# Three small moves in a TensorE-bound kernel: q of one more batch by DMA transpose, 1/rms of three batches spread by a DRAM round trip, and a new instruction order

## The chip, the cores and the metric

The kernel runs on one core of one Trainium2 chip. The metric is the device time of one execution in microseconds (us), the median over several runs. Each run also has a span (first to last instruction in the profile) and a mean granted TensorE clock. The profile of one run is shown in each case. Runs of the same kernel mostly differ by 1 to 3 us, and their mean clocks differ with them (one run of before took 207.58 us at a mean clock of 0.995, most about 210.5 at 0.96). In the job of the last four runs of the table further down, that one quick run makes three of the eleven runs of before count as slow (over 1.5% above the fastest). They are left out, which raises the ratios of these four runs by about 0.2%.

## The reference, cut to what matters

```python
def _attn_ref(q, k, v, g_norm):                 # 8 batches, 8 heads, 576 positions, 64 wide
    kv  = einsum('bhsd,bhse->bhde', k, v)
    out = einsum('bhsd,bhde->bhse', q, kv)
    rms = sqrt(mean(out * out, axis=-1) + 1e-06)
    return out / rms * g_norm

def _moe_ref(x, mu_k, mu_r, w_k, w_v, w_r):     # x: (8, 576, 512), w_k: 512x1024, w_v: 1024x512, w_r: 512x512
    xk = mu_k * x + (1 - mu_k) * x_prev         # x_prev: x one position earlier
    xr = mu_r * x + (1 - mu_r) * x_prev
    k  = maximum(xk @ w_k, 0)
    return sigmoid(xr @ w_r) * (k * k @ w_v)
```

Inputs and output are float32; the kernel computes in bfloat16 with float32 accumulation.

## The kernel before

Work is cut into named pieces. `add("K1.3", {"PE": ...}, fn, deps, bufs)` declares one; nothing is issued yet. A string, `ORDER`, then lists all pieces, with the engine (`:A` ScalarE, `:D` VectorE, `:S` SyncE) and the buffer slots where there is a choice. Each engine issues its pieces in exactly that order, and waits for what a piece needs. So a piece whose data is late holds up everything behind it on the same engine.

The names: for batch `b`, `load_q{b}` brings q in, `qT` transposes it on TensorE (PE) and `qTd` by DMA, `kv` is kᵀv, `u` is q·kv, `sq` squares it, `st` sums squares (PE), `rs` takes 1/sqrt (ScalarE), `sp` spreads the result over partitions (PE), `x` multiplies, `d`/`t`/`xk`/`xr` do the shift and blend. For group `g` of 512 tokens, `K`, `R`, `V` are the three products (four 128x512 matmuls a piece, 0.86 us), `o` the final multiplication and `S` the stores. `idle:28:0` is 28 matmuls on zeros, into a free slot, to keep PE active while the first loads come.

```python
    DMA_T = 3
    BUFS = {..., "sq": (1, (128, NHP, S), BF16), "rs": (2, (128, S), BF16), ...,
            "ps": (4, (128, 2, 512), FP32)}            # [cut]: buffers per tag; ps is PSUM

    # q of batch b
    if b >= DMA_T:                                      # batches 3 to 7: DMA transpose, issued by SyncE
        m = add(f"qTd{b}", {"SP": 7.5}, q_dma, bufs=[qin, qT], deps=[loaded[("q", b, 0)]], land=3.0)
        qts = {hp: m for hp in range(NHP)}
    else:                                               # batches 0 to 2: PE transposes into PSUM, then a copy
        ...

    # 1/rms, and its spread over the 64 partitions of each head
    st = add(f"st{b}", {"PE": 0.25}, st_mm, deps=sqs + [p_ones], bufs=[pst, sq], mode=3)
    rp = add(f"rs{b}", {"ACT": 0.54}, st_rs, deps=[st], bufs=[pst, rs], mode="norm")
    for half in range(2):
        m = add(f"sp{b}.{half}", {"PE": 0.125}, sp_mm, deps=[rp, p_sel], bufs=pp + [rs], mode=4)
        for i in range(2):
            x = add(f"x{b}.{half}.{i}", {"DVE": 0.67}, x_mul, deps=[m, ...], bufs=[pp[i], uT, xT])

    # stores: all row runs of 128 rows in one piece, on SyncE (last group: or ScalarE)
    def store(eng, g, ci, ot, cs): ...
```

## Time and profile before

| | before |
|---|---|
| median of 3 runs | 211.44 us (210.72 to 211.59) |
| span of the profiled run | 207.6 us |
| PE busy | 195.7 us (94%) |
| last matmul ends / tail after it | 200.96 / 6.66 us |

The profiled run of before (209.39 us) was quicker than its timed runs.

The first fence is the page of before. Its lines give busy time per engine, then busy tenths in 40 slices of 5.2 us (PEclk is the granted clock in tenths), then the chain that ended last, and two groups of instructions.

```profile
span 207.6 us, 3798 instructions
PE 195.7 (94%) x1526; PEld 93.9 (45%) x1526; DVE 141.1 (68%) x262; ACT 122.0 (59%) x146; POOL 28.7 (14%) x45
...
PE   7598999999999999999999999999999999999970
...
PEclk9955999999999999999999999999999999999998
...
PE 88%; DMA 3%; ACT 2%; POOL 2%; DVE 1%; issue 1%; POOLq 0%
...
L535 DVE TENSOR_TENSOR xT<-uT,ps 128x576 bf16<-128x576 bf16 x28 | 20.1, 751 | 6.4 <-PE ps L530 6.4
...
L276 POOL DMA_DIRECT2D q<-in_q_dram x12 | 8.6, 720 | 60.4 <-DMA qT<-q 39.2
```

PE is nearly full from the fifth slice to the tail, and the chain is PE. The PEclk strip shows the head at half clock (11.3 to 21.5 us in the trace). The line of L535 is the multiplication by the spread 1/rms, 0.75 us each, which the change replaces for three batches. The waits view of before for PE: total us, times, longest.

```profile
PE ps L401 <- DMA q<-in_q_dram: 2.1, 3, 1.5
PE ps L702 <- DVE zeros L227: 1.2, 1, 1.2
PE ps L476 <- ACT sq L192: 0.7, 1, 0.7
```

All of that lies in the head. The tile view of before for qT shows the transposes (count, then shortest, median and longest time that SyncE was held issuing one, in ns, then the starts):

```profile
L389 SPq DMA_TRANSPOSE qT<-q x5: 3002/8986/12377, 46.8 to 121.9; - x5
```

The one of 3.0 us is the last, when no loads ran. Four issued beside loads held SyncE for 8 to 12 us.

### The profile page before, as it was taken

The numbers are of one execution on the slowest core, as the hardware profiler recorded it, in microseconds if no ns is written. First come the engines' busy times: TensorE is split into PE (matmuls) and PEld (weight loads), VectorE is DVE, ScalarE is ACT, GpSimd is POOL, SyncE is SP. The second block draws the span as 40 slices with busy tenths as digits, with TensorE's granted clock in tenths as the row PEclk, the third lists the DMA queues.
The fourth block names the chain that finished last, engine by engine and source line by source line (L and its number), as shares of the span: only waits on it lengthen the run. The fifth ranks groups of instructions, "written<-read, shape, count | busy, mean of one in ns | idle before, by whom it ended". The sixth has DMA issues, their size and how long they took to land.

```text
span 207.6 us, 3798 instructions
## 1 busy us (share of the span) xinstructions
PE 195.7 (94%) x1526; PEld 93.9 (45%) x1526; DVE 141.1 (68%) x262; ACT 122.0 (59%) x146; POOL 28.7 (14%) x45
## 2 busy tenths in 40 slices
PE   7598999999999999999999999999999999999970
PEld 6443455444344534444854544444344444444440
DVE  1268728996788899998577997896848736322420
ACT  4567768287928798838956368456884045471010
POOL 7893301033000340001020000000000000000000
PEclk9955999999999999999999999999999999999998
DMA  6999999999999999999999348403200003603185
GB/s 156 188 200 204 204 203 206 203 149 183 182 145 191 213 277 231 163 191 266 113 160 213 88 107 196 117 0 82 73 0 0 0 3 93 214 0 91 42 232 144
DMA packets 39301, 29.71 MB, mean 143 GB/s; under 512 B 13548, under 2 KB 34804, under 8 KB 39284
## 3 DMA queue, kind: packets, MB, share of 16 engines
q0 software_dynamic: 21232, 16.48, 52.9%
q1 hardware_dynamic: 17516, 12.43, 28.3%
q10 hardware_dynamic: 536, 0.56, 0.9%
q8 instruction: 12, 0.20, 0.4%
q14 instruction: 5, 0.04, 0.1%
HBM read 33.56 MB, written 9.44 MB: 207 GB/s over the span
## 4 chain that ended last, share of the span: by engine, by line
PE 88%; DMA 3%; ACT 2%; POOL 2%; DVE 1%; issue 1%; POOLq 0%
PE ps L655 31%; PE ps L599 30%; PE ps L621 16%; DMA v<-in_v_dram 3%; PE ps L348 3%; PE ps L431 2%; PE ps L363 2%; PE ps L530 2%; POOL q L276 1%; PE ps L514 1%; PE ps L425 1%; PE ps L476 1%; ACT relu L603 1%; ACT L200 1%; DVE xr L566 0%
## 5 line engine op out<-in xcount | busy, mean ns | idle before, releaser
L599 PE MATMUL ps<-xk,w_k 128*128 128x512 bf16 (+1 forms) x320 | 67.4, 358 | 0.0
L655 PE MATMUL ps<-w_v,sqk 128*128 128x512 bf16 (+1 forms) x296 | 66.6, 374 | 0.0
L603 ACT ACTIVATE relu<-ps 128x1024 bf16<-128x1024 f32 x36 | 36.6, 1023 | 25.4 <-PE ps L599 23.5
L599 PEld LDWEIGHTS <-w_k 128*128 128x128 bf16 x320 | 30.1, 98 | 29.9 <-issue 1.6
L655 PEld LDWEIGHTS <-sqk 128*128 128x128 bf16 x296 | 27.6, 98 | 31.9 <-issue 1.1
L606 DVE TENSOR_TENSOR sqk<-relu 128x1024 bf16<-128x1024 bf16 x36 | 24.5, 687 | 21.2 <-ACT relu L603 21.1
L621 PE MATMUL ps<-w_r,xr 128*128 128x512 bf16 x144 | 35.5, 389 | 0.1
L659 DVE TENSOR_TENSOR out<-ps,sig 128x1024 f32<-128x1024 f32 (+2 forms) x21 | 22.3, 1069 | 11.5 <-PE ps L655 9.0
L626 ACT ACTIVATE sig<-ps 128x1024 bf16<-128x1024 f32 x18 | 18.1, 1022 | 16.8 <-PE ps L621 16.7
L535 DVE TENSOR_TENSOR xT<-uT,ps 128x576 bf16<-128x576 bf16 x28 | 20.1, 751 | 6.4 <-PE ps L530 6.4
L186 ACT ACTIVATE t<-d,mu_sb 128x576 bf16<-128x576 bf16 x23 | 16.4, 767 | 13.1 <-DVE d L556 13.1
L621 PEld LDWEIGHTS <-xr 128*128 128x128 bf16 x144 | 13.7, 100 | 17.8 <-issue 1.8
L276 POOL DMA_DIRECT2D q<-in_q_dram x12 | 8.6, 720 | 60.4 <-DMA qT<-q 39.2
L188 DVE TENSOR_SCALAR t<-d,mu_sb 128x576 bf16<-128x576 bf16 x41 | 13.5, 372 | 0.2
L180 ACT CAST uT<-ps 128x576 bf16<-128x576 f32 x16 | 9.9, 640 | 6.2 <-PE ps L431 5.3
L556 DVE TENSOR_TENSOR d<-xT 128x1152 bf16<-128x1152 bf16 (+1 forms) x18 | 12.4, 692 | 0.6
L182 DVE CAST uT<-ps 128x576 bf16<-128x576 f32 x12 | 9.1, 755 | 5.0 <-PE ps L425 3.8
L566 DVE TENSOR_TENSOR xr<-t,xT 128x1152 bf16<-128x1152 bf16 (+1 forms) x18 | 12.3, 687 | 0.2
L566 DVE TENSOR_TENSOR xk<-t,xT 128x1152 bf16<-128x1152 bf16 (+1 forms) x18 | 11.8, 687 | 0.3 <-ACT t L186 0.2
L276 POOL DMA_DIRECT2D k<-in_k_dram x11 | 7.9, 715 | 12.8 <-PE ps L348 10.7
L200 ACT ACT_TABLE_LOAD x7 | 9.0, 1283 | 0.8 <-PEq L719 0.7
L626 ACT ACT_TABLE_LOAD x7 | 9.0, 1283 | 0.1
(60 smaller groups left out, 125.1 us busy)
## 6 DMA issues: line engine op xcount, KB each, us to landing
out_dram<-out SPq DMA_DIRECT2D x23, 192.0 KB
q<-in_q_dram POOLq DMA_DIRECT2D x6, 576.0 KB, 14.2
v<-in_v_dram POOLq DMA_DIRECT2D x6, 576.0 KB, 15.6
k<-in_k_dram POOLq DMA_DIRECT2D x6, 576.0 KB, 17.4
out_dram<-out SPq DMA_DIRECT2D x24, 128.0 KB
out_dram<-out SPq DMA_DIRECT2D x23, 64.0 KB
w_k<-in_moe_w_k_dram POOLq DMA_DIRECT2D x2, 512.0 KB, 11.7
w_v<-in_moe_w_v_dram POOLq DMA_DIRECT2D x2, 512.0 KB, 17.0
```

Source lines behind the costliest of these rows:

```text
L186: nc.scalar.mul(out=dst, in_=src, mul=by)
L188: nc.vector.tensor_scalar_mul(out=dst, in0=src, scalar1=by)
L276: nc.gpsimd.dma_start(out=get(kvq[(n, b)])[:, h0:h1, :], in_=rows(n, b, h0, h1))
L535: nc.vector.tensor_tensor(out=get(xT)[:, 2 * i:2 * i + 2, NP + c:NP + c + HS], in0=flat(slice(2 * i, 2 * i + 2))[:, :, c:c + HS], in1=get( ...
L566: nc.vector.tensor_tensor(out=dst[:, hsl, c0:c0 + S], in0=get(t[key])[:, hsl, :], in1=get(xT)[:, hsl, 0:S], op=ALU.add)
L599: nc.tensor.matmul(get(ps)[:, fc % 2, a0:a1], w_k_sb[:, cc, 128 * fc:128 * fc + 128], xk[:, cc, x0:x0 + a1 - a0], start=(cc == 0), stop=(c ...
L603: nc.scalar.activation(out=get(rt), in_=get(ps), func=AF.Relu)
L606: nc.vector.tensor_mul(out=get(sqk)[:, 2 * f2:2 * f2 + 2, :], in0=get(rt), in1=get(rt))
L621: nc.tensor.matmul(get(ps)[:, ci % 2, :], xr[:, cc, c:c + 128], w_r_sb[:, cc, :], start=(cc == 0), stop=(cc == NHP - 1))
L626: nc.scalar.activation(out=get(sg), in_=get(ps), func=AF.Sigmoid)
L655: nc.tensor.matmul(get(ps)[:, ci % 2, cs], get(sqk)[:, fc, 128 * ci:128 * ci + 128], w_v_sb[:, fc, cs], start=(fc == 0), stop=(fc == NFC - 1))
L659: nc.vector.tensor_mul(out=get(ot)[:, xs, cs], in0=get(ps)[:, xs, cs], in1=get(sg)[:, xs, cs])
```

## The change

The intent is to take work from PE: four transposes of batch 2's q, and six spreads (two for each of batches 5 to 7). The order was made anew with a model in which loads and transposes share the DMA engines. Three smaller things come with it: w_r is loaded in two halves, the stores of the last two groups are split by row run over two issuing engines, and pieces of batch 1 move ahead of the first `R`. The diff, cut to its core:

```diff
-    DMA_T = 3
+    DMA_T = 2
+    SPREAD = 5
+    dram = ctx.enter_context(tc.tile_pool(name="dram", bufs=1, space=bass.MemoryType.DRAM))
+    scratch = {b: dram.tile([H, S], BF16, name=f"scratch{b}") for b in range(SPREAD, B)}
...
-            for half in range(2):
+            if b >= SPREAD:
+                def rs_out(eng, rs=rs, rows8=rows8):
+                    (nc.sync if eng == "SP" else nc.scalar).dma_start(out=rows8, in_=get(rs)[0:128:16, :])
+                def rs_in(eng, rows8=rows8):
+                    for e in range(2):
+                        (...).dma_start(out=get(sq)[64 * e:64 * e + 64], in_=rows8.rearrange("(h e) s -> e h s", e=2)[e:e + 1].broadcast_to([64, NHP, S]))
+                def x_stt(_, i):
+                    nc.vector.scalar_tensor_tensor(out=get(xT)[:, hsl, NP:NP + S], in0=flat(hsl), scalar=g_col, in1=get(sq)[:, hsl],
+                                                   op0=ALU.mult, op1=ALU.mult)
+                wr = add(f"rw{b}", ..., rs_out, deps=[rp], bufs=[rs], land=0.08)
+                rd = add(f"rr{b}", ..., rs_in, deps=[wr], bufs=[sq], land=1.6)
+                for i in range(2):
+                    x = add(f"x{b}.{i}", {"DVE": 1.27}, x_stt, deps=[rd, ...], bufs=[sq, uT, xT])
+            for half in range(2 if b < SPREAD else 0):
...
-    p_wr = add("load_w_r", ...)
+    p_wr = [add(f"load_w_r{i}", ...) for i in range(2)]
...
+                    for i, part in enumerate([rows] if g < NG - 2 else [[r] for r in rows]):     # stores S7, S8: one piece a row run
...
 ORDER = """ [all of it is new; the parts that matter:]
-    ... R0.0 ... kv1.0 ... qT1.3 qT1.2 ...
+    ... qT1.0 ... qT1.1 ... qT1.3 ... qT1.2 ... kv1.0 ... R0.0 R0.1 R0.2 ...
-    ... qT2.1 qT2.0 st1 ... qT2.2 ... qT2.3 ... kv2.0 ... u2.3 ...
+    ... load_w_v1 ... load_q2.0 ... V0.1a qTd2 ... kv2.0 ... R1.3 ... u2.2 u2.3 ... R1.2 ...
+    ... K4.5 ... rw5 rr5 ... R4.2 ... x5.1 ... V4.3b x5.0 ... sq6.0 sq6.1 st6 ... kv7.0 ... V4.2b K5.5 ...
```

## The prediction

> **What bounds the kernel now.** TensorE. On the profile's page PE is busy 195.7 of 207.6 us; the table of stretches shows it busy every microsecond from 20 to 200 except 0.7 us near 31 and 36. The chain of waits is 88% PE. Outside that dense part lie the head (first r matmul at 19.3 us, paced by loads that land every 0.74 us per two heads, at a granted clock of 0.50 from 11.3 to 21.5 us) and the tail (last matmul ends at 201.0, SyncE issues its last store at 203.9, the span ends at 207.6). VectorE (68%) and ScalarE (59%) have room. So only PE work removed, or a wait added in front of PE, moves the time.
>
> **Removed from PE's dense part** (start-to-start times in the timeline): four PE transposes of batch 2's q, 0.26 to 0.35 us each: about 1.2. Six spreads of batches 5 to 7, 0.23 each, plus 0.10 us by which a plain matmul group is longer before such a tiled group (0.96 against 0.86): about 2.0. The new order also moves two batch-1 transposes and half of its kv (0.28, 0.28, 0.79) ahead of the first r group. That group now waits for the first half of w_r, which comes behind four more batch-1 loads: by the landing rate about 20.5 us instead of 19.3, so the head gives part back. Net: about 3.4 us less. Storing the last groups row run by row run, split over SyncE and ScalarE, shortens SyncE's backlog: perhaps 0.8 us.
> The DRAM round trip (8 rows out, two broadcast reads in) is off the chain: I estimate 5 to 7 us from rs to x, and the order leaves that distance. VectorE: two fused multiplies (estimate 1.2 us each) for four of 0.75; about even.
>
> **Added.** Batch 2's q goes by DMA transpose in the middle of the load stream. In the trace, transposes issued under loads took long: issued at 46.8, first packets at 51.9, done near 66; issued at 77, done near 94; without loads (121.9) 4.4 us. Each is 2,304 packets of 256 B; during loads the trace shows them alternating one for one with 768 B load packets (about 141 of each per 0.75 us). That agrees with the Trainium skill, "DMA: Bandwidth & Descriptors", "Queues, rings and completion order": round robin per packet. So it needs about 5 us to its first packet and 12.3 us after. Batch 2's q lands behind the same bytes as w_v before (38.1) plus one load of 2.9: about 41. The transpose is done near 58. The new order puts batch 2's first u matmul after group 0's v, four K groups, kv2 and one R group: PE gets there near 48. I expect PE to stand still there about 10 us (DMA qT<-q), nothing to fill it, since its queue is in order. After that gap the clock falls to half, as in the head ("TensorE: Matmul & The Clock Gate", "The HAM clock gate"): about 1.5 us more. Later transposes have slack.
>
> **Sum.** 211.4 - 3.4 - 0.8 + 10 + 1.5 = about 218.5. Predicted 218.5 us, range 210 to 222; faster by over 2%: 0.08, within 2%: 0.19, slower: 0.73.
>
> **Right if:** waits list PE's u matmuls of batch 2 behind DMA qT<-q for 8 to 12 us around 48 to 58 us; the granted clock drops there; afterwards PE is dense to the end; no PE wait on the broadcast reads; PE's total busy time falls by 2 to 4 us.
>
> **Wrong if:** the transpose gets past the loads faster than in the trace of before (done by 50: then about 207), or q lands earlier; or the stall is shared with kv2; or the round trip is late and K of groups 5 to 7 waits, which adds to the time.

## The result, and the profile after

| | before | after |
|---|---|---|
| median of 3 runs | 211.44 us | 220.08 us (219.86 to 220.63) |
| ratio | | 1.0423 (95%: 1.0376 to 1.0471) |
| span of the profiled run | 207.6 us | 217.8 us |
| PE busy | 195.7 us | 195.5 us |
| first `R` starts | 19.31 us | 23.63 us |
| first `K` of group 1 starts | 44.40 us | 45.95 us |
| last matmul ends / tail | 200.96 / 6.66 us | 212.25 / 5.56 us |

A ratio here and below is the mean time of one kernel's runs over the mean of the other's from the same rounds, so not quite the ratio of the medians quoted beside it. The changed kernel is slower. The same lines of the page, after:

```profile
span 217.8 us, 3746 instructions
PE 195.5 (90%) x1495; PEld 95.0 (44%) x1495; DVE 140.5 (65%) x251; ACT 120.8 (55%) x147; POOL 29.6 (14%) x46
...
PE   7758799994199999999999999699999999999990
...
PEclk9995999999679999999999999999999999999999
...
PE 67%; DMA 14%; SPq 5%; DVE 4%; ACT 3%; POOL 3%; issue 2%; DVEq 0%; ACTq 0%; POOLq 0%
PE ps L685 23%; PE ps L629 23%; PE ps L651 13%; DMA qT<-q 8%; DMA v<-in_v_dram 3%; SPq L615 3%; PE ps L436 2%; DMA scratch<-rs 2%; PE ps L353 2%; POOL q L280 2%; SPq L394 1%; DMA out_dram<-out 1%; ACT L204 1%; PE ps L558 1%; PE ps L406 1%
...
L543 DVE SCALAR_TENSOR_TENSOR xT<-uT,mu_sb,sq 128x1152 bf16<-128x1152 bf16 x6 | 8.5, 1414 | 4.0 <-DMA sq<-scratch 3.9
```

Two places stand out in the PE strip: the digits 4 and 1 (about 49 to 60 us) and a single 6 (136 to 142 us). The clock strip falls just after the first. The chain of waits, 88% PE before, now contains the DMA transpose (8%), SyncE's queue, and the write of 1/rms to DRAM. The waits of PE name both places (first and third line); the second is the wait for batch 0's v in the head, the fourth stands right behind the first `R` piece:

```profile
PE ps L436 <- DMA qT<-q: 7.4, 1, 7.4
PE ps L368 <- DMA v<-in_v_dram: 2.5, 2, 2.0
PE ps L519 <- ACT sq L196: 1.7, 2, 0.9
PE ps L651 <- DVE xr L594: 1.4, 1, 1.4
```

**First place.** This is PE's timeline after (start, duration, engine, line, operation; in brackets the idle time before it and what ended it):

```profile
50.39 1.03 PE L651 MATMUL ps<-w_r,xr 128*128 128x512 bf16 x4
58.86 0.69 PE L436 MATMUL ps<-qT,kv 64*64 64x288 bf16 x8 [7.45 <-DMA qT<-q]
59.49 1.89 PE L651 MATMUL ps<-w_r,xr 128*128 128x512 bf16 x4
```

PE finished an `R` piece at 51.4 us and stood until 58.86 for batch 2's transposed q. An `R` piece, four matmuls, took 1.03 us before the gap and 1.89 after it. In before, batch 2's first `u` piece followed the piece ahead of it without a gap:

```profile
50.66 0.44 PE L431 MATMUL ps<-qT,kv 64*64 64x288 bf16 x8
```

The table of stretches of after for PE (stretch, length, busy us and instructions, granted clock, DMA share, GB/s) shows the reason for the slow piece:

```profile
53.00:58.00 5.00, 0.00 (x0) 0.83 1.53 136
58.00:63.00 5.00, 4.14 (x23) 0.50 1.29 195
```

In the trace the clock was at half from 56.30 to 63.12 us. SyncE issued this transpose at 41.21 us, just after q of batch 2 landed at 41.07. From 45.5 to 53 us the records of the DMA engines show the transpose's 256 B packets and the load queue's packets (768 B, but for a few of 4 B) in equal numbers: 284 against 284, 280 against 283, 286 against 285, 286 against 285, 276 against 279 in successive stretches of 1.5 us. With no transpose beside them, from 40.5 to 43.5 us, the loads passed about 397 in 1.5 us: they are slowed too.

**Second place.** First VectorE's timeline after, then PE's, in the same columns:

```profile
127.66 1.28 DVE L636 TENSOR_TENSOR sqk<-relu 128x1024 bf16<-128x1024 bf16 x2
132.85 1.42 DVE L543 SCALAR_TENSOR_TENSOR xT<-uT,mu_sb,sq 128x1152 bf16<-128x1152 bf16 x1 [3.91 <-DMA sq<-scratch]
```

```profile
137.93 0.30 PE L519 MATMUL ps<-sq,ones 128*32 128x288 bf16 x2 [0.92 <-ACT sq L196]
138.99 0.42 PE L519 MATMUL ps<-sq,ones 128*32 128x288 bf16 x6 [0.75 <-ACT sq L196]
```

1/rms of batch 5 was ready at 123.95 us. The write was issued at 123.97, the two reads at 127.61 and 128.36, and the first multiply that uses them started at 132.85: 8.9 us for the round trip. VectorE, in order, stood 3.9 us. `x5.0` ended at 136.64, which freed the `sq` buffer; only then could ScalarE square batch 6 (136.72 to 138.94), and PE waited for those squares at `st6`.

**The sum.** On PE's own time line the end moved by 11.3 us (200.96 to 212.25). Compared piece by piece, start to start:

| where | us |
|---|---|
| head and batch 2's transposes, up to the first `K` of group 1 | +1.55 |
| wait for `qTd2` | +7.45 |
| half clock after that wait (`u2`, `R1.2`, `K1.1`) | about +1.9 |
| batch 5's round trip (`V4.3b` to `K5.5`: 0.98 + 1.04 + 0.17) | +2.2 |
| everything else, the six spreads included (what is left) | about -1.8 |

The tail then gave back 1.1 us. The head entry is the net of 1.2 us of removed transposes and about 1.35 us of batch 1's pieces that now stand ahead of the first `R` (both by the prediction's counts), and of a first `R` that began 4.3 us later. That `R` did not wait for its weights: the first half of w_r landed at 20.61 us, while PE was busy with the pieces ahead of `R` from 15.60 to 23.63 us, with one gap of 0.74 us, and at half clock until 22.16.

### The profile page after: what moved, and what is told of

Same layout as the page of the kernel before. It is cut to its first block, busy times and chain, and to the rows that moved or that the text cites. A ratio compares the mean times of both kernels' runs of the same rounds, so it can differ in the third digit from the quotient of the medians.

```text
span 217.8 us, 3746 instructions
## 1 busy us (share of the span) xinstructions
PE 195.5 (90%) x1495; PEld 95.0 (44%) x1495; DVE 140.5 (65%) x251; ACT 120.8 (55%) x147; POOL 29.6 (14%) x46
## 4 chain that ended last, share of the span: by engine, by line
PE 67%; DMA 14%; SPq 5%; DVE 4%; ACT 3%; POOL 3%; issue 2%; DVEq 0%; ACTq 0%; POOLq 0%
PE ps L685 23%; PE ps L629 23%; PE ps L651 13%; DMA qT<-q 8%; DMA v<-in_v_dram 3%; SPq L615 3%; PE ps L436 2%; DMA scratch<-rs 2%; PE ps L353 2%; POOL q L280 2%; SPq L394 1%; DMA out_dram<-out 1%; ACT L204 1%; PE ps L558 1%; PE ps L406 1%
## 5 line engine op out<-in xcount | busy, mean ns | idle before, releaser
L685 PE MATMUL ps<-w_v,sqk 128*128 128x512 bf16 (+1 forms) x296 | 65.9, 374 | 0.0
L633 ACT ACTIVATE relu<-ps 128x1024 bf16<-128x1024 f32 x36 | 36.1, 1023 | 25.2 <-PE ps L629 17.8
L685 PEld LDWEIGHTS <-sqk 128*128 128x128 bf16 x296 | 28.1, 98 | 32.4 <-issue 0.9
L190 ACT ACTIVATE t<-d,mu_sb 128x576 bf16<-128x576 bf16 x29 | 20.8, 768 | 17.9 <-DVE d L584 17.9
L280 POOL DMA_DIRECT2D v<-in_v_dram x11 | 7.9, 714 | 48.0 <-PE ps L353 37.5
L563 DVE TENSOR_TENSOR xT<-uT,ps 128x576 bf16<-128x576 bf16 x16 | 11.4, 750 | 1.9 <-PE ps L558 1.7
L436 PE MATMUL ps<-qT,kv 64*64 64x288 bf16 x96 | 5.8, 320 | 7.4 <-DMA qT<-q 7.4
L192 DVE TENSOR_SCALAR t<-d,mu_sb 128x576 bf16<-128x576 bf16 x35 | 11.3, 366 | 0.3
L543 DVE SCALAR_TENSOR_TENSOR xT<-uT,mu_sb,sq 128x1152 bf16<-128x1152 bf16 x6 | 8.5, 1414 | 4.0 <-DMA sq<-scratch 3.9
## 6 DMA issues: line engine op xcount, KB each, us to landing
k<-in_k_dram POOLq DMA_DIRECT2D x6, 576.0 KB, 11.3
```

Source lines behind the costliest of these rows:

```text
L190: nc.scalar.mul(out=dst, in_=src, mul=by)
L280: nc.gpsimd.dma_start(out=get(kvq[(n, b)])[:, h0:h1, :], in_=rows(n, b, h0, h1))
L563: nc.vector.tensor_tensor(out=get(xT)[:, 2 * i:2 * i + 2, NP + c:NP + c + HS], in0=flat(slice(2 * i, 2 * i + 2))[:, :, c:c + HS], in1=get( ...
L633: nc.scalar.activation(out=get(rt), in_=get(ps), func=AF.Relu)
L685: nc.tensor.matmul(get(ps)[:, ci % 2, cs], get(sqk)[:, fc, 128 * ci:128 * ci + 128], w_v_sb[:, fc, cs], start=(fc == 0), stop=(fc == NFC - 1))
```

## The experiments

Theories that the runs were to tell apart: (A) `qTd2` is late because its packets share the DMA engines with loads; (B) such a transpose takes that long in any case; (C) the wait at `u2` hides a lack of other inputs; (D) most of the loss lies in the round trip and the head; (E) the round trip costs time on PE, with the rival that it does not; (F) the first `R` is late because batch 0's last v lands late; (G) it is late because of the chain of small steps at half clock ahead of it, not because of loads; (H) the half clock after the wait costs about 1.9 us. Medians of before in the three jobs were 210.86, 210.71 and 210.41 us.

| run | base | median us | ratio to before (95%) |
|---|---|---|---|
| gate | after | 214.09 | 1.0156 (1.0103 to 1.0208) |
| early_q2 | after | 216.43 | 1.0236 (1.0141 to 1.0331) |
| pe_q2 | after | 213.23 | 1.0103 (1.0066 to 1.0141) |
| before_qTd2 | before | 216.80 | 1.0299 (1.0234 to 1.0363) |
| pe_q2_zero_rt | pe_q2 | 210.44 | 0.9975 (0.9952 to 0.9999) |
| pe_q2_rtfix | pe_q2 | 212.47 | 1.0068 (1.0040 to 1.0095) |
| pe_q2_head | pe_q2 | 212.07 | 1.0059 (1.0035 to 1.0082) |
| before_tail | before | 208.39 | 0.9896 (0.9852 to 0.9940) |
| after_idle | after | 218.95 | 1.0426 (1.0360 to 1.0493) |
| after_fixed | after | 212.31 | 1.0124 (1.0055 to 1.0193) |
| before_tail_idle | before | 207.89 | 0.9895 (0.9846 to 0.9945) |
| before_tail_rt7 | before | 209.52 | 0.9972 (0.9916 to 1.0027) |

### gate: no loads beside the transpose

```diff
+ add("gate", {"POOL": 0.1}, lambda _: nc.gpsimd.tensor_copy(out=gate_sb, in_=get(qT)[0:1, 0, 0:1]), deps=[m], bufs=[qT])   # b == 2
- ... K1.0 load_v3.0 load_k3.0 ... V1.2b V1.3b load_q3.0 qTd3
+ ... K1.0 gate load_q3.0 load_v3.0 load_k3.0 ... V1.2b V1.3b qTd3
```

GpSimd issues the loads; one tiny copy from the transposed q makes it hold back batch 3's loads until `qTd2` has landed.

> The changed kernel, with one edit: a tiny GpSimd copy that reads batch 2's transposed q stands in front of the loads of v3, k3 and q3 (q3 first), so no load shares the DMA engines with batch 2's transpose once v2 has landed. Theory A (the transpose is slow because its 2,304 packets alternate one for one with load packets): it is issued near 41 as before, is done near 48 to 49 instead of 58.5, the 7.4 us wait of PE on DMA qT<-q at batch 2 is gone, the clock does not fall at 56; batch 3's q comes later, so up to 3 us of a new wait at batch 3's u; time 211 to 214 us. Rival B (the transpose takes 15 us or more by itself, whatever runs beside it): still done after 55, the wait stays at 7 us or more, time 219 to 222.

This is GpSimd's timeline of gate, then PE's:

```profile
46.74 0.18 POOL L399 COPY gate<-qT 1x1 bf16<-1x1 bf16 x1 [20.42 <-DMA qT<-q]
```

```profile
50.12 1.03 PE L652 MATMUL ps<-w_r,xr 128*128 128x512 bf16 x4
51.08 0.44 PE L437 MATMUL ps<-qT,kv 64*64 64x288 bf16 x8
...
72.36 0.44 PE L437 MATMUL ps<-qT,kv 64*64 64x288 bf16 x8 [2.58 <-DMA qT<-q]
```

The transpose was issued at 41.41 us as before and landed by 46.74: 5.3 us instead of 17.6. Its first packet came 1.3 us after its issue (4.0 us in after). In the records 1,370 of its packets passed between 44.5 and 46.0 us, about five times the rate beside loads. PE ran into batch 2's `u` without a gap and at full clock. So A holds and B falls. What the later loads cost is the last line: batch 3's own transpose, issued at 53.88, now came 2.6 us late. Still the ratio to before fell from 1.0423 to 1.0156 (the medians by 6.0 us).

### early_q2: the same transpose, earlier

```diff
- load_w_k1 ... load_w_v1 ... load_q2.0 ... V0.1a qTd2
+ load_w_k1 load_q2.0 ... qTd2 st1 ... load_w_v1
```

> The changed kernel with batch 2's q loaded five loads' worth earlier: its load stands directly behind the second half of w_k, ahead of w_v and k2, and its transpose stands earlier in SyncE's order; nothing else moves. Theory A (the wait is a start time of 41 plus about 17 us under loads, against PE's arrival at 51): the transpose is issued near 33, still takes 16 to 18 us, is done near 50, and PE's wait at batch 2's u falls from 7.4 to under 1 us; the second half of w_v now comes behind it and is slowed, which costs 1 to 2 us before the v of group 0; up to 2 us at batch 3's u; time 212 to 215. Rival C (the wait at batch 2's u is only where a lack of other inputs shows, for example kv2's loads): the time stays at 218 or more.

The transpose was issued at 33.45 us, and PE waited only 0.49 us for it at 52.52. The direction is as A says, and the ratio fell from 1.0423 to 1.0236. It fell less than expected (216.43 us against 212 to 215). A wait that was allowed for with up to 2 us came out longer: PE's timeline of this run.

```profile
73.98 0.69 PE L434 MATMUL ps<-qT,kv 64*64 64x288 bf16 x8 [2.82 <-DMA qT<-q]
```

That is batch 3's transpose, and the clock was at half from 73.6 to 77.0 us. In after the same piece did not wait, because PE reached it only at 79.3 us. The slack of the later transposes was lateness of PE.

### pe_q2: batch 2's q by PE again

```diff
- DMA_T = 2
+ DMA_T = 3
- qTd2
+ qT2.2 qTc2.2:D qT2.3 qTc2.3:A kv2.0 ... qT2.1 qTc2.1:D qT2.0 qTc2.0:A R1.2
```

> The changed kernel with one part undone: batch 2's q is transposed on PE again (four groups of six transposes and four copies out of PSUM, put around kv2), all else kept. Theory A: the 7.4 us wait and the half clock after it go, 1.2 us of transposes come back, some 1 us of PSUM waits; time 211 to 213.5, about the kernel before. That leaves nothing over for the other parts together (head, round trip, tail). Rival D (the round trip and the head lose most of the time and the wait at u2 would only move): 216 or more.

As expected: the wait at `u2` is gone, PE is dense from 26 to 128 us apart from fractions of a microsecond, and the time is 213.23 us. With transposes on PE the new order is 1.0% slower than before; with the DMA transpose it is 4.2% slower. So this one part is worth about 3% of loss.

### before_qTd2: only the DMA transpose, in the old order

```diff
- DMA_T = 3
+ DMA_T = 2
- qT2.1 ... qT2.0 ... qT2.2 ... qT2.3 (and their copies)
+ qTd2 st1
```

> The kernel before with one part of the change alone: batch 2's q by DMA transpose, in the old order, where q2 lands near 33 and PE comes to batch 2's u at 50.7. Theory A: the transpose runs 33 to 50 under loads, so it is just in time; PE is spared four transposes (1.2 us), loads of w_v, v2 and k2 are delayed by about 3 us each and cost up to 1 us; time 210 to 212 (ratio to before 0.995 to 1.003). Rival B (a DMA transpose in the load stream costs the PE 7 us or more wherever it stands): 217 or more.

This was a miss. The transpose was issued at 33.78 us and `u2` did not stall, as expected, but the kernel took 216.80 us (ratio 1.0299). That is almost rival B's number, but not by B's path. PE's timeline of this run:

```profile
78.49 1.49 PE L346 MATMUL ps<-v,k 96*64 96x64 bf16 x48 [3.67 <-DMA v<-in_v_dram]
79.91 3.59 PE L597 MATMUL ps<-xk,w_k 128*128 128x512 bf16 x8
```

Batch 4's v came 3.7 us late, and eight matmuls of `K` then took 3.59 us instead of 1.90, since the clock was at half from 77.2 to 84.0. In this kernel the transposes were not late, but the loads were: GpSimd waited 52.2 us for transposes to free q's buffers (39.2 us in before). The load of batch 4's q shows it. It needs the buffer of batch 2's q, which PE's transposes left in time for the load to be issued at 44.86 us in before; here it waited for `qTd2` until 51.95. The loads behind it in GpSimd's order wait with it. Batch 4's v was issued at 54.99 us instead of 49.96 and landed at 78.36 instead of 70.21, so 5.0 of its 8.2 us of lateness were there at the issue. How much of the rest is the sharing of the DMA engines is not separated. From the first `K` of group 1 to `V4.3b` this run lost 6.2 us more than before did. Another 2.9 us of its profiled run lie in a head at half clock until 26 us, which the other three runs seem to share only in part (mean clocks 0.951 to 0.958, against 0.937); that part is not explained.

### pe_q2_zero_rt: the round trip taken out

The result is wrong (relative error 0.61): the DRAM write and reads are dropped, and the fused multiplies take what lies in `sq`, the squares.

```diff
- wr = add(f"rw{b}", ...); rd = add(f"rr{b}", ...)
+ x deps: [rp, ...]                     # and no rw/rr in ORDER
```

> Wrong result on purpose. The kernel pe_q2 (the change with batch 2's q on PE again, 213.23 us, ratio 1.010) with the DRAM round trip taken away and nothing put in its place: for batches 5 to 7 the fused multiply reads the squares that lie in the same buffer, so no write, no read, no wait; all else kept. It gives the most that a round trip without latency could give. Theory E (the round trip is not off the chain: about 9 us from rs to the first fused multiply for batch 5 hold VectorE, then ScalarE, then PE at st6, kv7 and the K of group 5, 3.2 us in pe_q2's trace): the waits of PE around st6 go, time 2 to 3.3 us lower, ratio to before 0.995 to 1.001. Rival (the round trip is off the chain, as I predicted; the waits at st6 come from something else): within 0.6 us of pe_q2, ratio 1.007 to 1.013.

From pe_q2 to this run the ratio falls from 1.0103 to 0.9975: 1.3%, about 2.7 us. `st6` follows without a wait, as PE's timeline of pe_q2 and then of this run shows:

```profile
130.24 0.30 PE L518 MATMUL ps<-sq,ones 128*32 128x288 bf16 x2 [0.93 <-ACT sq L195]
```

```profile
129.64 0.43 PE L518 MATMUL ps<-sq,ones 128*32 128x288 bf16 x8
```

So E holds: in this order the round trip costs more than the removal of six spreads gains (2.0 us by the prediction's count). It also gives a bound: with the DMA transpose undone and a round trip that took no time at all, this order would be only 0.25% quicker than before.

### pe_q2_rtfix: a second buffer for the squares

```diff
- "sq": (1, ...)
+ "sq": (2, ...)                       # slots alternate by batch
- ... tk5.2 ... xr5.2 ... sq6.0 sq6.1 st6
+ ... sq6.0 sq6.1 tk5.2 ... st6
```

> The kernel pe_q2 with two buffers instead of one for the squares, which the broadcast is read into, and with the squares of batch 6 ahead of batch 5's mu multiply in ScalarE's order, so that batch 6's norm does not stand behind batch 5's round trip. Theory E with the chain over the single buffer and ScalarE's order: the 2.0 us of PE waits at st6 and kv7 go; what stays is K of group 5 waiting for batch 5 itself (up to 1.5 us); time 0.7 to 2 us below pe_q2, ratio 1.001 to 1.007. If only the latency to K5 counts and not the buffer: within 0.4 us of pe_q2.

The wait at `st6` is gone, but only a part of the time: 1.0068, between pe_q2 and zero_rt (its interval overlaps that of pe_q2). The run changes two things, the buffer and the place of the squares in ScalarE's order, and does not tell them apart. PE's timeline of this run shows the rest:

```profile
132.24 1.04 PE L628 MATMUL ps<-xk,w_k 128*128 128x512 bf16 x4
134.72 6.20 PE L628 MATMUL ps<-xk,w_k 128*128 128x512 bf16 x28 [1.45 <-DVE out L688]
```

VectorE stood 3.5 us for the broadcast reads (3.9 in after). The output multiplication `o4.0`, which comes behind `x5` and the blends on VectorE, was late by that much, and its PSUM buffer was the one that the next `K` pieces needed. So the round trip reaches PE by two paths: the `sq` buffer, and VectorE's queue through PSUM. This run closes only the first.

### pe_q2_head: batch 0's last loads first

```diff
- load_q1.0 load_q0.2 ... load_v0.6 load_q1.4      qT1.0 ... kv0.1 ... kv0.3
+ load_q0.2 ... load_v0.6 load_q1.0 load_q1.4      kv0.1 ... kv0.3 qT1.0
```

> The kernel pe_q2 with batch 1's two q loads moved behind all loads of batch 0 (and the one PE transpose that needs them behind the kv of batch 0): undoes a part of the new load order. Theory F (the head is late because batch 0's last v lands at 15.5 instead of near 13.9 behind a load of batch 1): the first r matmul group starts 1.2 to 2 us earlier than 23.6, time lower by 1 to 2 us, ratio 1.000 to 1.006. Rival G (the head is bounded by the chain of small PE, ScalarE and VectorE steps at half clock, not by loads): the start moves by under 0.5 us, time within 0.5 us of pe_q2.

`kv0.3` moved from 15.47 to 14.27 us, but the first `R` stayed: 23.87 us against 23.62. Its profile times are to be read with care; that the first `R` did not come earlier is all that is taken from it. PE then waited 1.0 us for q of batch 1 instead. The ratio improved by 0.4%, and the intervals overlap. This favours G (the late `R` is not set by those loads), but it is thin evidence. What fills PE from 16 to 23.6 us in after includes batch 1's transposes and `kv1.0`, most of it at half clock, and G's own test, taking those pieces back behind `R0`, was not run.

### before_tail: only the split stores, in the old kernel

The diff is the `runs`/`store` part of the change, with the stores of groups 7 and 8 in `ORDER` split and dealt to SyncE and ScalarE.

> The kernel before with one part of the change alone: the stores of the last two groups row run by row run, split over SyncE and ScalarE. In before the last store was issued 3 us after the last matmul and the span ended 6.6 us after it; in after 5.6 us. Expected: the tail from the last matmul to the end shrinks by 0.8 to 1.5 us, time 209.4 to 210.2, ratio 0.993 to 0.997. Rival (the tail is the landing of the last store, not SyncE's backlog): ratio 0.998 to 1.002.

This beats both kernels: 208.39 us, 0.9896, a gain of 1.0% (clear of the noise, more than the 0.993 to 0.997 that was expected). SyncE's timeline in before and in this run:

```profile
195.38 9.02 SPq L581 DMA_DIRECT2D out_dram<-out  x14
```

```profile
197.10 4.74 SPq L587 DMA_DIRECT2D out_dram<-out  x7
```

In before SyncE issued 14 stores, 0.64 us each, until 204.4 us, 3.4 us after the last matmul, and ScalarE only 4. Now it issues 7 in that stretch, until 201.84, and ScalarE as many. The tail shrank from 6.66 to 4.67 us; the last matmul did not move (201.01 us).

### after_idle: PE kept active during the wait

```diff
- u2.2 u2.3
+ idle:60:2 u2.2 u2.3
```

> The changed kernel with 60 idle matmuls on zeros (0.097 us each at full clock, 5.8 us) put in PE's order just ahead of batch 2's first u, that is inside the 7.4 us in which PE stands still; nothing else. They can't shorten the wait, whose end is the landing of the transpose near 58.5. Theory H (after the wait the granted clock is 0.5 from 56 to 63 us, which costs about 1.9 us): the clock stays at 1.00 across 50 to 63 us, the groups after the wait take 0.86 instead of up to 1.8 us, time 1.5 to 2.2 us below after's 220.08, ratio to before 1.030 to 1.036. Rival: the half clock comes whatever PE does there, or costs nothing; within 0.5 us of 220.08.

By the ratio nothing was gained: 1.0426 against 1.0423. But the interval (1.0360 to 1.0493) reaches to the forecast of 1.030 to 1.036, three runs of before are left out here, and the median is 1.1 us below that of after, so a gain of about 1 us is not excluded. The profile shows that the local gain was there and that most of it was lost again. PE's timeline of this run:

```profile
51.49 5.91 PE L733 MATMUL ps<-zeros 128*128 128x224 bf16 x60
58.89 0.44 PE L434 MATMUL ps<-qT,kv 64*64 64x288 bf16 x8 [1.49 <-DMA qT<-q]
...
136.49 0.30 PE L517 MATMUL ps<-sq,ones 128*32 128x288 bf16 x2 [1.52 <-ACT sq L194]
```

The clock stayed full through the wait (from 22.6 to 138.7 us), `u2.2` took 0.44 us instead of 0.69, and `V4.3b` began 1.84 us earlier than in after, 2.1 earlier counted from the first `K` of group 1. So the half clock did follow from PE's idleness, and it did cost about 2 us there. But at batch 5's round trip this run lost 3.8 us (`V4.3b` to `K5.5`) where after lost 2.2. The waits for the squares were longer by 0.6 us, and they brought a half clock from 138.7 to 142.1 us. The last matmul ended at 211.99 us against 212.25. The traces show why the clock fell there in this run and not in after. Within one trace all its changes before the tail lie a multiple of 3.41 us apart. Cut into windows by this grid, PE was busy 42% of the window before the fall in this run (135.27 to 138.68 us). In after the waits fell into two windows, and PE was busy 73 and 78% of them. After 26 us, over all fourteen traces, the clock fell behind seven windows with PE busy 0 to 52% and never behind a busier one; one window of 52% (in this run, with the idle matmuls in and before it) did not bring a fall. pe_q2, where the clock fell too (132.8 to 136.2 us), had 52% there, and pe_q2_rtfix, where it did not, 55%.

### after_fixed: the three repairs together

```diff
  pe_q2 + pe_q2_rtfix + pe_q2_head
```

> The changed kernel with three repairs together: batch 2's q on PE again (pe_q2), two buffers for the squares with batch 6's squares ahead on ScalarE (rtfix), batch 1's q loads behind batch 0's (head). If the parts add up: ratio 1.0103 - 0.0035 - 0.0044 = 1.0024, between 1.000 and 1.005. So all that the change was meant to gain would be eaten even then by the later head, and only the tail stays as a gain.

The repairs did not add up: 1.0124, with an interval that contains the ratios of pe_q2, pe_q2_rtfix and pe_q2_head alike. The waits for v in the head are gone, but PE waits for q of batch 1 instead (2.3 us in all, the longest 1.58 us at 15.57 us), the first `R` began at 24.62 us, and the stop of 1.4 us right after `K5.5`, for VectorE's `o4.0`, is there as in rtfix. A repaired wait was each time followed by the next one.

### before_tail_idle: more idle matmuls in the head

```diff
- idle:28:0 qT1.0 ... qT0.0 ... qT0.2 ... kv0.2 ... kv0.1
+ idle:42:0 qT1.0 ... idle:3:3 qT0.0 ... idle:3:1 qT0.2 ... idle:5:1 kv0.2 ... idle:4:2 kv0.1
```

> The kernel before_tail (208.39, ratio 0.990) with 29 more idle matmuls in the head where PE waits for loads (14 more in front, four groups of 3 to 5 between the first transposes and kv), another thing that the new order does. If PE's business in those 3.4 us windows is what holds the clock, it stays at 1.00 for longer than up to 11.3 us and R0 runs at full clock: 0.5 to 2 us less, ratio 0.981 to 0.988. If not: within 0.3 us, or 0.3 us worse for matmuls that come late.

The half clock in the head shrank from 10.24 us to 3.41 in the profile, and the mean granted clock of all six runs rose to 0.985 to 1.000 (before_tail: 0.955 to 0.975). The ratio, 0.9895, is that of before_tail. The first `R` started at the same 19.22 us, so the full clock ahead of it gained nothing, and the half clock that was left (19.9 to 23.3 us) lay on the first `R` pieces. The times lay closer together (207.17 to 208.34 us, against 207.16 to 209.97), but a gain is not shown.

### before_tail_rt7: the round trip for the last batch alone

Here no loads run any more, and the order leaves room.

```diff
+ SPREAD = 7
- ... rs7 ... sp7.1 ... x7.1.1 x7.1.0 ... sp7.0 ...
+ ... rs7 rw7:S rr7:S ... x7.0 d7.0 x7.1 d7.2 ...
```

> The kernel before_tail with the DRAM round trip for the last batch alone, where no load is under way and 14 us lie between its norm and the first matmul that needs it. PE is spared two spreads (0.66 us with the lengthening before them); from the traces I work out that the round trip and the fused multiplies bring x of batch 7 so late that the first K of group 8 waits 0.5 to 1 us. Expected: no gain, ratio to before 0.988 to 0.993 (before_tail 0.990). Rival (the distance is enough): 0.986 to 0.988.

No gain is seen: 0.9972 against 0.9896, with intervals that overlap. VectorE waited 1.8 us for the reads, and PE 1.56 us at the first `K` of group 8. PE's timeline of this run:

```profile
168.72 0.59 PE L627 MATMUL ps<-xk,w_k 128*128 128x512 bf16 x2 [1.56 <-DVE xk L592]
```

Two spreads removed are worth about 0.7 us, from the prediction's costs, so the wait is enough to take it all. (This profile also had a head at half clock until 25 us, which the other kernels show in some runs too.)

## Why the prediction was right or wrong

Direction and size held: 218.5 us predicted, 220.08 measured, and slower as given the most weight. The mechanism named first, the wait for the transpose, is the one that the runs show. That the size fits so well is in part luck. Term by term, on the profiles, the head came out 2.9 us worse than its share of the sum (+1.55 at the first `K` of group 1, where the prediction's counts give about -1.35), the round trip 2.2 us worse, and the wait 2.55 us better. The head and the wait cancel for a reason, given below. The round trip is a plain miss, and part of it does not show, because the profiled run of before was quicker than its median: the spans grew by 10.2 us, the medians by 8.6, and 7.1 was predicted.

- **The bound: right.** PE bounds before; apart from the tail, only what was put in front of PE moved the time.
- **The wait for batch 2's transpose: right in cause, place and end.** Given as "done near 58"; PE went on at 58.86. The counting of packets, one for one with the loads, is what the records show (284 against 284). The gate run shows the cause by taking the loads away. This agrees with the Trainium skill, "DMA: Bandwidth & Descriptors", "Queues, rings and completion order", which says that the engines go round robin between queues, packet by packet.
- **Its size: a term mis-sized.** PE came to it at 51.4 us, not "near 48", so the wait was 7.45 us, not 10 (and below the "8 to 12" given under "Right if"). The reason is the head: the first `R` began at 23.6 us, not "about 20.5". The prediction let `R` start when w_r landed, and w_r did land then (20.61), but PE still had the pieces ahead of `R` to do, at half clock. The two errors cancel in the sum, because the end of the wait is set by the DMA and not by PE. The head's loss is simply paid inside the wait.
- **Half clock after the gap: right.** Half from 56.3 to 63.1 us, about 1.9 us lost there against 1.5 predicted. After_idle shows that PE's idleness caused it. The half-clock stretches in all these traces, but for the last one of each, which the end of the run cuts, last 3.41 us or a multiple (6.83, 10.24, 17.07), which agrees with the free-running window of 3,413 ns in the Trainium skill, "TensorE: Matmul & The Clock Gate", "Part 1: The HAM clock gate".
- **"The DRAM round trip ... is off the chain: I estimate 5 to 7 us from rs to x, and the order leaves that distance", with "no PE wait on the broadcast reads": the step that failed.** It took 8.9 us, and it reached PE by two paths that the estimate did not look for: the single `sq` buffer held until `x5` is done, and VectorE's queue, whose standing still keeps PSUM from being freed. It costs about 2.7 us (pe_q2 against zero_rt), more than the 2.0 that the six spreads were worth. The prediction had named this as a way of being wrong, but not put it into the sum. The Trainium skill, "DMA: Bandwidth & Descriptors", "Anatomy of one DMA", gives about 2 us of fixed cost for a DMA issued by GpSimd. Two of that kind in a row would be 4, as an estimate; these were issued by SyncE, for which that section gives no figure. Here the reads could be issued only 3.6 us after the write beside a load (123.97 to 127.61), and 1.8 us after it for batch 7, when no loads ran (160.18 to 162.01).
- **"PE's total busy time falls by 2 to 4 us": wrong.** It went from 195.7 to 195.5. The new order has 45 idle matmuls instead of 28, and matmuls at half clock are busy longer (1.89 us against 1.03 for four). Busy time was the wrong thing to watch; the sum of gaps on PE's time line is the right one.
- **"Later transposes have slack": right in after, and only there.** It was the 7.45 us of lateness. In gate and early_q2, where PE was not late, batch 3's transpose was 2.6 and 2.8 us behind.
- **Tail: right.** 0.8 us predicted, 1.1 measured, and 2.0 when done alone in the old kernel.
- **Fused multiply:** 1.41 us against an estimate of 1.2. For two that is 2.8 against 3.0 us for four of 0.75: even, as said.

So the expected 3.4 us of removed PE work went this way. The 1.2 us of transposes and the pieces of batch 1 moved forward were more than paid back by the late head (net +1.55 us at the first `K` of group 1). The 2.0 us of spreads were paid back at `st6` and behind `K5.5`. On top came the wait for the transpose and its clock. What stays open: which part of the new head costs how much, why the last 300 packets of `qTd2` took from 54.5 to 57.9 us, and why the clock in the head stays at half for one, two, three or five windows of 3.41 us.

## What to carry to other kernels

Before moving work from a bounding engine to a DMA, count the packets that will share the DMA engines at that moment, in both directions: a transpose of 2,304 packets took 5.3 us alone and 17.6 us beside loads, and where it was in time it made the loads late instead, most of all by holding the buffer that the next load needed. A detour through DRAM is "off the chain" only if every buffer it holds and every in-order queue that waits for it has room for it too; here both the buffer and VectorE's queue led back to PE. Look also at the cheap parts of a large change one by one: splitting the last stores over two issuing engines, alone, gave 1.0%, and it was the only part that paid when tested.

## What the Trainium skill lacked or had wrong

- "DMA: Bandwidth & Descriptors", "Latency and other measured facts", gives a DMA transpose 261 GB/s where the middle dimension is not contiguous. Alone it came close (gate: 1,370 packets of 256 B in 1.5 us, 234 GB/s). Beside loads it was 48 GB/s (280 packets in 1.5 us), and neither this nor the slowing of the loads is on the page, though its rule of round robin leads there.
- The same page, "Anatomy of one DMA", gives about 2 us fixed for a DMA issued by GpSimd, and none in that section for one issued by SyncE. A DRAM write followed by dependent reads took 8.9 us from the end of the producer to the start of the consumer beside other traffic, and `qTd2` in after had its first packets only about 4 us after its issue (41.2 to about 45) while loads were under way, against 1.3 us in gate (41.41 to 42.68), where the last load was just ending. No page gives this delay behind loads.
- "TensorE: Matmul & The Clock Gate", "What's actually happening", has half clock after an idle window and full clock after a busy one. Here it fell behind windows of 3.41 us in which PE was still busy 29% (early_q2), 42% (after_idle) and 52% (pe_q2). In the head of before the clock was at half from 11.3 to 21.5 us, three such windows, with PE busy 100, 92 and 83% of them, by small matmuls and transposes; with 29 more idle matmuls half clock lasted 3.4 us. "Part 4: PE-mode transpose" says that transposes don't count as busy in the same way, which would fit, but no run here tests it.
- No page gives a time for the fused scalar_tensor_tensor in bfloat16: 1.41 us for 128x1152, against 0.69 to 0.76 us for a tensor_tensor of that shape.
